# First batch's spectral rows moved inside SBUF, convolution sums seeded in PSUM, transposes in one pass: a Fourier and mlp kernel on one core

## The chip, the cores and the metric

The kernel runs on one core of one Trainium2 chip, in one launch. The metric is the device time of one execution in microseconds (us). Times were taken over three runs of the kernel before: median 1088.05, lowest 1087.7, highest 1088.87. One further execution was profiled; its span is 1087.9 us, and all durations below come from it.

The core has five engines that work from instruction streams of their own: TensorE (PE; its weight loads are listed as PEld), VectorE (DVE), ScalarE (ACT), GpSimd (POOL), and SyncE (SP), which here issues the transfers. Each runs its instructions in a fixed order and waits on semaphores for the others. Matmul results land in PSUM banks; everything else lives in SBUF or in DRAM.

## The reference, cut to what matters

```python
def _attn_ref(x, weight_gen):               # B=8, S=4224, D=192, H=8 heads, K=7 taps
    w = exp(weight_gen - max); w = w / (sum(w) + 1e-09)        # softmax over the taps
    x_pad = np.concatenate([np.zeros((B, K - 1, D)), x], axis=1)
    x_unf = x_pad[:, np.arange(S)[:, None] + np.arange(K)[None, :], :].reshape(B, S, K, H, D // H)
    return np.einsum('bshk,bskhg->bshg', w, x_unf).reshape(B, S, D)

def _moe_ref(x, w_ch1, w_ch2):
    X = np.fft.fft(np.fft.fft(x, axis=1), axis=2)
    u = x + np.real(X)
    un = (u - mean(u)) / np.sqrt(var(u) + 1e-06)               # over the last axis
    return u + np.maximum(un @ w_ch1, 0.0) @ w_ch2             # 192 -> 768 -> 192
```

The second function is applied to what the first returns. Everything is fp32 in and out.

## The kernel before

A batch of 4224 rows is held as 128 partitions by 33 rows of 192 values. The 33 rows are cut into eight chunks of four rows (0 to 7) and one chunk (8) of one row; after the transform the rows are worked on in nine groups. A batch goes through these stages:

- `conv` (`wide_conv` from batch 2 on): the softmax of the taps, and for each chunk seven products of the input rows with the tap weights and their sum. In batch 0 chunks 0, 1, 3, 5 and 7 are summed on TensorE: each product tile `pr` is multiplied by an fp32 identity into a pair of PSUM banks `pa` (L767, and L732 for the products that ACT makes, L723), and ACT copies the banks to `u` (L779). The other chunks and batches add `pr` to `u` on POOL or DVE (L771). The constants `PE_SUMS`, `ACT_TAPS`, `POOL_TAPS`, `DVE_ADDS` say which engine makes and adds which tap; batch 0's chunks are taken in the groups `[(8,0), (1,2), (3,4), (5,6), (7,)]`.
- `fold` (L794, L795) adds two mirrored halves of a chunk into `sm` on POOL. `spectrum` takes a 128-point transform of `sm` on TensorE (`pg`, L803), ACT copies a part (`up`), and DVE writes sums and differences as `gt` (L810, L813). `gt` has 128 partitions, the cosine and sine parts of 65 frequencies. SP stores it in DRAM as `g_d` (L816, L817).
- `transform` loads `g_d` back in pieces `g` of four frequency triples, 102 partitions each (L889, L891), and takes the 33-point transform on TensorE (`pp`, L899); ACT copies the result to `pq`.
- `mix`: for each group four pairs of matmuls (`eo`, L930), a copy on ACT (`ot`), and four DVE operations that add the result to `u` (L936 to L939).
- `norm`: for the first three groups of batch 0 (`QUICK = 3`) the statistics come from DVE (L960, L961), ACT normalises (`un`, L976), TensorE transposes by a matmul with the fp32 identity (`tr`, L986), ACT copies the high half to fp16 (`ht`, L987), and DVE subtracts for the low half (L989). For all other groups POOL makes the two halves (`hl`, L1001, L1003), and a DMA transposes them (L1006).
- `mlp`: `ph` (L1060) is the first matmul into 768 columns, ACT and DVE evict it with the relu, `po` (L1094) is the second, and DVE evicts it onto `u` (L1099). Group g of batch 0 has `po_g_0` and `po_g_1`, one for each half of its rows. The weights are loaded and split into fp16 parts (batch 0's weight preparation: `words_to_f32`, L472 to L483, and `split_f32`, L488, L489, on ACT and DVE).

Nothing of this is scheduled by hand. `kernel` traces all instructions once, `plan` gives each a price by `cost` (TensorE by columns and passes, a transfer by its issue, its landing and its queue time), and `walk` lists them: at each step the instruction that opens next on its engine, ranked by what hangs behind it. The result is one static order for each engine, so a changed price or a changed instruction shifts the order of much else. Warm-up matmuls (`keep_warm`) are put where TensorE has nothing else; `WARM` says after which group and how many.

The tables of the 33-point transform (`te`, `to`) and of the 128-point transform (`f1`) fix in which partition a frequency lands.

## Time and profile before

| | |
|---|---|
| median of 3 runs | 1088.05 us (1087.7 to 1088.87) |
| span of the profiled execution | 1087.9 us |
| TensorE busy / weight loads | 1065.5 / 802.9 us |
| DVE, ACT, POOL busy | 958.7, 800.0, 857.1 us |
| granted TensorE clock, mean | 0.998 |
| TensorE idle, 0 to 60 us | 9.2 us |
| TensorE idle, 200 to 1000 us | 3.5 us |
| first `ph` of group 0 | at 100.68 us |
| first instruction that issues the store of the last `gt` of batch 0 | at 71.45 us |

The profiled execution ran 0.15 us shorter than the median. Of the stages, batch 0's convolution lasts to about 71 us, its transform to 90, and its first mlp matmul begins at 100.7. The convolution of batch 1 lies beside batch 0's mlp and ends on POOL at 199.6 us. From there to 1000 us TensorE is idle less than 1% of the time.

A row of a timeline gives the start and the length in us, the engine, the line, the operation, what it writes and reads, how many such instructions follow one another, and in brackets the idle time before the first of them and what ended it. A row of a group of instructions gives the count, the busy time in us, the mean duration of one in ns, and the idle time before them. Rows of waits give total us, times, longest.

### The profile page before, as it was taken

What the parts mean: (1) busy time and instruction counts of PE and PEld (TensorE: products, weight loads), DVE (VectorE), ACT (ScalarE), POOL (GpSimd) and SP (SyncE); (2) the same over time, 40 slices, a digit from 0 to 9 for tenths busy, and PEclk for the clock granted to TensorE, in tenths of its full rate; (3) what the DMA queues carried; (4) which work ended last, traced back from release to release, by engine and by line L of the source; (5) the groups of instructions that cost most, each with busy time, mean ns of one, the idle gap of its engine ahead of it and who ended that gap; (6) DMA issues with size and microseconds to landing.
All of it is one profiled execution on the core that took longest, in us unless ns stands there. A gap on an engine that the chain in (4) does not pass through costs nothing.

```text
span 1087.9 us, 23453 instructions
## 1 busy us (share of the span) xinstructions
PE 1065.5 (98%) x8600; PEld 802.9 (74%) x8600; DVE 958.7 (88%) x1639; ACT 800.0 (74%) x2414; POOL 857.1 (79%) x615
## 2 busy tenths in 40 slices
PE   7899999999999999999999999999999999999998
PEld 5477777787767877777778876887778777786767
DVE  8999999899989999899999999899999998355543
ACT  4666864679966878788786877678786878588842
POOL 5989699899969999799969999699969999011200
PEclk9999999999999999999999999999999999999999
DMA  9353135714492348623582348624582333623311
GB/s 323 129 146 115 34 94 141 202 46 111 119 259 80 85 115 206 170 67 85 129 248 79 92 109 220 157 57 121 122 205 68 83 68 89 140 56 76 79 53 48
DMA packets 171091, 131.20 MB, mean 121 GB/s; under 512 B 119067, under 2 KB 151776, under 8 KB 170976
## 3 DMA queue, kind: packets, MB, share of 16 engines
q1 hardware_dynamic: 170976, 129.70, 45.2%
q8 instruction: 68, 1.11, 0.4%
q14 instruction: 47, 0.39, 0.1%
HBM read 61.46 MB, written 39.37 MB: 93 GB/s over the span
## 4 chain that ended last, share of the span: by engine, by line
PE 66%; DVE 14%; POOL 5%; DMA 4%; ACT 3%; issue 3%; SPq 0%; DVEq 0%; ACTq 0%; POOLq 0%
PE po L1094 27%; PE ph L1060 24%; PE pp L899 5%; PE eo L930 4%; PE ph L1027 3%; DVE pr L847 3%; POOL u L771 2%; PE pg L803 2%; DVE hh L1080 2%; ACT pr L723 1%; DMA ht<-hl 1%; DVE pr L762 1%; POOL u L851 1%; DMA g<-g_d 1%; DMA ring<-ht 1%
## 5 line engine op out<-in xcount | busy, mean ns | idle before, releaser
L851 POOL TENSOR_TENSOR u<-u,pr 128x1536 f32<-128x1536 f32 x144 | 497.0, 3452 | 5.5 <-DVE pr L847 1.7
L1094 PE MATMUL po<-w2h,hh 128*128 128x192 f16 x2832 | 409.2, 247 | 0.0
L1094 PEld LDWEIGHTS <-hh 128*128 128x128 f16 x4248 | 359.1, 98 | 60.1 <-issue 15.2
L1060 PE MATMUL ph<-ht,w1h 128*128 128x512 f16 (+1 forms) x1296 | 382.7, 362 | 0.3 <-ACT ht L987 0.3
L1094 PE MATMUL po<-w2l,hh 128*128 128x192 f16 x1416 | 348.8, 246 | 0.0
L1080 DVE SCALAR_TENSOR_TENSOR hh<-ph,hh 128x512 f16<-128x512 f32 (+1 forms) x390 | 240.5, 636 | 60.9 <-ACT hh L1079 60.5
L1079 ACT ACTIVATE hh<-ph 128x512 f16<-128x512 f32 (+1 forms) x390 | 206.0, 550 | 89.2 <-PE ph L1060 41.0
L847 DVE TENSOR_TENSOR pr<-x_sb,wp 128x1536 f32<-128x1536 f32 x144 | 249.7, 1747 | 7.3 <-POOL u L851 7.3
L1060 PEld LDWEIGHTS <-w1h 128*128 128x128 f16 x1296 | 125.3, 98 | 97.9 <-issue 9.4
L1060 PE MATMUL ph<-ht,w1l 128*128 128x512 f16 (+1 forms) x528 | 181.7, 350 | 0.0
L996 ACT ACTIVATE un<-u,rs 128x192 f32<-128x192 f32 x252 | 122.2, 539 | 40.2 <-POOL rs L994 34.5
L1001 POOL TENSOR_TENSOR hl<-un,hl 128x512 f16<-128x512 f32 (+1 forms) x69 | 74.9, 1086 | 84.3 <-issue 42.5
L771 POOL TENSOR_TENSOR u<-u,pr 128x768 f32<-128x768 f32 (+1 forms) x72 | 117.9, 1649 | 12.2 <-DVE pr L762 11.4
L967 ACT ACTIVATE junk<-u,st 128x192 f16<-128x192 f32 x252 | 114.3, 453 | 4.4
L965 ACT ACTIVATE junk<-u 128x192 f16<-128x192 f32 x252 | 90.8, 360 | 27.6 <-DVE u L939 21.8
L1099 DVE SCALAR_TENSOR_TENSOR u<-po,isc,u 128x384 f32<-128x384 f32 (+1 forms) x122 | 73.1, 599 | 21.1 <-PE po L1094 20.7
L930 PEld LDWEIGHTS eo<-cs_sb,pq 97*128 97x128 f32 x544 | 78.3, 191 | 13.4 <-issue 4.4
L930 PE MATMUL eo<-cs_sb,pq 97*128 97x97 f32 x544 | 85.7, 275 | 0.0
L762 DVE TENSOR_TENSOR pr<-x_sb,wp 128x768 f32<-128x768 f32 (+1 forms) x91 | 74.7, 868 | 2.1 <-POOL u L771 0.7
L1060 PEld LDWEIGHTS <-w1l 128*128 128x128 f16 x528 | 51.9, 98 | 21.6 <-issue 0.5
L794 POOL TENSOR_TENSOR sm<-u 128x382 f32<-128x382 f32 x64 | 64.6, 1009 | 3.7 <-ACT u L779 3.2
L994 POOL TENSOR_TENSOR rs<-st,rs 128x4 f32<-128x4 f32 (+1 forms) x69 | 13.6, 201 | 67.4 <-DVE rs L970 67.3
(130 smaller groups left out, 1538.4 us busy)
## 6 DMA issues: line engine op xcount, KB each, us to landing
out_dram<-u SPq DMA_DIRECT2D x64, 384.0 KB
x_sb<-in_x_dram SPq DMA_DIRECT2D x48, 384.0 KB
g<-g_d SPq DMA_DIRECT2D x40, 336.0 KB
x_sb<-in_x_dram SPq DMA_DIRECT2D x8, 864.0 KB
g_d<-gt SPq DMA_DIRECT2D x32, 195.0 KB
g_d<-gt SPq DMA_DIRECT2D x32, 189.0 KB
w<-in_weight_gen_dram SPq DMA_DIRECT2D x6, 924.0 KB
x_sb<-in_x_dram SPq DMA_DIRECT2D x8, 672.0 KB
```

What stands on the lines that cost most here:

```text
L762: last_product[b] = nc.vector.tensor_tensor(out=dst, in0=rows, in1=wk, op=ALU.mult)
L771: adder.tensor_tensor(out=u, in0=u, in1=pr, op=ALU.add)
L847: last_product[b] = nc.vector.tensor_tensor(out=pr.rearrange("p (s r) (h g) -> p s (r h) g", s=2, g=G), in0=rows, in1=wp[:, :, :, k:k + 1] ...
L851: nc.gpsimd.tensor_tensor(out=u, in0=u, in1=pr, op=ALU.add)
L930: last_mix[b] = nc.tensor.matmul(eo[:, e, j, :], lhsT=pq[0:DH, e, r, r:r + P], rhs=cs_sb[:, e, :], start=True, stop=True)
L965: nc.scalar.activation(junk, uv[t], AF.Identity, scale=-1.0 / D, accum_out=st[:, t, 0:1])
L967: nc.scalar.activation(junk, uv[t], AF.Square, bias=st[:, t, 0:1], accum_out=st[:, t, 1:2])
L996: nc.scalar.activation(un[:, t, :], uv[t], AF.Identity, bias=rs[:, 1, t:t + 1], scale=rs[:, 0, t:t + 1])
L1060: last_ph[n] = nc.tensor.matmul(ph[:, 0:T], lhsT=wt[:, cs_], rhs=ht[:, 0:T, blk], start=(i == 0 and not opens), stop=(i == len(terms) - 1 ...
L1079: nc.scalar.activation(a[:, 0:T], ph[:, 0:T], AF.Relu)
L1080: nc.vector.scalar_tensor_tensor(out=l[:, 0:T], in0=ph[:, 0:T], scalar=0.0, in1=a[:, 0:T], op0=ALU.max, op1=ALU.subtract)
L1094: nc.tensor.matmul(po[t // 2][:, t % 2, :], lhsT=hx[:, t], rhs=wx[:, c2, :], start=(c2 == 0 and i == 0), stop=(c2 == NH - 1 and i == len(t ...
```

## The change

In batch 0 the `gt` rows are no longer stored in DRAM and loaded again. They go from SBUF to SBUF: 17 transfers of 126 rows by 768 bytes and 18 small ones of one or two rows put them where `transform` reads them, into a part of the tile of batch 1's rows, which is not used yet. For this `u` becomes two fixed tiles (`halves`), the tables are put in the order 6 x 21 frequency rows and 2 left over, and batches 1 to 7 store `g_d` as [22, 6, 17, 192] in two transfers of 126 and 2 rows. The stores of zeros at the start are gone.

For each chunk summed on TensorE DVE's first product is written into the two PSUM banks, in two halves, after small fp16 identity matmuls have opened the banks; before, it was a product in SBUF and two fp32 identity matmuls.

The `norm` transposes of the first three groups use the transpose mode of TensorE. The groups of batch 0 become `[(8,0), (1,2), (3,4), (5,), (6,7)]`; ACT's tap of chunk 7 becomes a DVE product, and the folds of chunks 5 and 7 go to DVE, one operand of them read from PSUM. The warm-up after the last chunk has 18 matmuls in place of 40. `cost` has new prices: transposes of one pass, SBUF to SBUF transfers at 600 ns and 1.5 ns for each piece, slower DVE operations with two SBUF operands.

```diff
-ACT_TAPS = {(0, 1): (0,), (0, 3): (0,), (0, 5): (0,1), (0, 7): (0,)}
+ACT_TAPS = {(0, 1): (0,), (0, 3): (0,), (0, 5): (0,1)}
-WARM = {-1: 14, 7: 40}
+WARM = {-1: 14, 6: 18}
+DVE_FOLDS = (5, 7)
+OPENING = [(8, 0), (1, 2), (3, 4), (5,), (6, 7)]
...
-        t = 2 * max(112 if 64 < n <= DH else 56, 0.855 * n) if reads[0].dtype == F32 else max(55.8, 0.417 * n + 2.4)
+        t = (1 if ins.is_transpose else 2) * max(112 if 64 < n <= DH else 56, 0.855 * n) if reads[0].dtype == F32 else max(55.8, 0.417 * n + 2.4)
...
-        return 400, 2000 + WIRE * count(out) * size, out.ap[0][1] * count(out) / run * (0.5 + 0.0023 * run * size)
+        local = all(ap.tensor.name in sbuf for ap in reads + writes)
+        return 600 + 1.5 * out.ap[0][1] * count(out) / run if local else 400, 2000 + WIRE * min(map(count, reads + writes)) * size, out.ap[0][1] * count(out) / run * (0.5 + 0.0023 * run * size)
...
-        t = 150 + (6.27 if ins.opcode == "Reciprocal" else 1.042) * n + (60 if len(reads) == 3 and n < 512 else 0)
+        slow = len(reads) == 2 and n > 64 and all(ap.tensor.name in sbuf and ap.ap[-1][0] for ap in reads)
+        t = 150 + (6.27 if ins.opcode == "Reciprocal" else 2.0 if slow else 1.042) * n + (60 if len(reads) == 3 and n < 512 else 0)
...
+    halves = [cpool.tile([P, NC // 2, 8, D], F32, name=f"u{i}") for i in range(2)]
+    g0 = halves[1][:, 1:NC // 2].rearrange("p q r d -> p (q r) d")
+    ident16 = ident32.bitcast(F16)[:, 0:P]
...
-                    if i > 0 or pa:
+                    seeds = pa if i == 0 and mine else None
+                    if seeds:
+                        for bank in seeds:
+                            for at_ in range(0, 2 * D, P):
+                                nc.tensor.matmul(bank[:, at_:at_ + P], lhsT=ident16, rhs=ident16, start=(at_ == 0), stop=False)
+                    elif i > 0 or pa:
...
+                        if seeds:
+                            for h in range(2):
+                                last_product[b] = nc.vector.tensor_tensor(
+                                    out=pa[h][:, 0:2 * D].rearrange("p (n g) -> p n g", g=G), in0=rows[:, h], in1=wk[:, h], op=ALU.mult)
...
+                    if pa and c in DVE_FOLDS:
+                        fold(b, sm, pa[0][:, 0:2 * D].rearrange("p (r d) -> p r d", r=2), u[:, 1], nc.vector)
...
-        if at == 2 or c == NC:
+        if b == 0:
+            for j in range(J):
+                last_g2[0] = nc.sync.dma_start(g0[t2 + j:t2 + j + 6 * NT:NT, 0:NM], gt[0:6 * NM, at + j])
+            for kk in range(2):
+                last_g2[0] = nc.sync.dma_start(g0[kk * NT + t2:kk * NT + t2 + J, NM], gt[6 * NM + kk:6 * NM + kk + 1, at:at + J])
+        elif at == 2 or c == NC:
...
-                    nc.tensor.matmul(tr[i][0:m, t, :], lhsT=un[:, t, i * P:i * P + m], rhs=ident32, start=True, stop=True)
+                    nc.tensor.transpose(tr[i][0:m, t, :], un[:, t, i * P:i * P + m], ident32)
```

The first place is SP's order of transfers at the end of batch 0's convolution; before, two stores of the last `gt` and then the loads of the transform:

```order
L816 DMA g_d_95<-gt_4_452 65x768
L817 DMA g_d_95<-gt_4_452 63x768
L816 DMA g_d_95<-gt_6_591 65x768
L817 DMA g_d_95<-gt_6_591 63x768
L889 DMA g_0_0_716<-g_d_95 112x4x192
L889 DMA g_0_4_734<-g_d_95 112x4x192
L889 DMA g_0_8_752<-g_d_95 112x4x192
```

The same place after the change:

```order
L636 DMA x_sb<-in_x_dram 128x768
L846 DMA u_73<-gt_4_473 6x21x192 x4
L846 DMA u_73<-gt_6_658 6x21x192 x4
L848 DMA u_73<-gt_4_473 2x1x192 x4
L848 DMA u_73<-gt_6_658 2x1x192 x4
```

The loads are gone; four long transfers of each of the last two `gt` tiles and eight small ones stand in their place.

The second place is DVE around the first mix rows of group 0 (`eo_0`), which stood behind the preparation of the second weight's parts (`w2f`):

```order
L478 TENSOR_SCALAR pa_w_1_1014<-pw_w_1_1015 128x384
L481 SCALAR_TENSOR_TENSOR t_w_1_1016<-raw_w_416,pa_w_1_1014 128x384
L483 TENSOR_TENSOR w2f<-pw_w_1_1015,t_w_1_1016 128x384
L936 TENSOR_TENSOR eo_0_928<-eo_0_928,ot_0_933 128x2x97
L937 TENSOR_TENSOR eo_0_928<-eo_0_928,ot_0_933 128x194
L938 TENSOR_TENSOR u_0_145<-u_0_145,eo_0_928 128x2x2x97
```

After the change the same engine has:

```order
L486 SCALAR_TENSOR_TENSOR t_w_0_978<-raw_w_432,pa_w_0_976 128x384
L971 TENSOR_TENSOR eo_0_900<-eo_0_900,ot_0_905 128x2x97
L501 SCALAR_TENSOR_TENSOR w1l_90<-pw_w_01_889,sc_w_851,w1h_89 128x384
L972 TENSOR_TENSOR eo_0_900<-eo_0_900,ot_0_905 128x194
L487 TENSOR_SCALAR pa_w_0_976<-raw_w_432 128x384
L973 TENSOR_TENSOR u_72<-u_72,eo_0_900 128x2x2x97
```

The first mix moved ahead of most of that preparation (parts 0 and 1 of the second weight), which now stands between the mix rows.

The third place is TensorE at the first output matmul of group 1 (`po_1_0`). Before, the first `ph` of group 3 stands ahead of it:

```order
L1060 MATMUL ph_2_5_1439<-ht_2_1107,w1l_90 128x512
L1060 LDWEIGHTS w1h_87
L1060 MATMUL ph_3_0_1470<-ht_3_1277,w1h_87 128x512
L1060 LDWEIGHTS w1l_88
L1060 MATMUL ph_3_0_1470<-ht_3_1277,w1l_88 128x512
```

After the change it stands behind it, and `po_1_0` follows directly on the last `ph` of group 2:

```order
L1099 MATMUL ph_2_5_1410<-ht_2_1079,w1l_92 128x512
L1133 MATMUL po_1_0_1302<-w2f,hh_1_0_1176 128x192
L1133 MATMUL po_1_0_1302<-w2f,hh_1_1_1189 128x192
L1133 MATMUL po_1_0_1302<-w2f,hh_1_2_1223 128x192
L1133 MATMUL po_1_0_1302<-w2f,hh_1_3_1237 128x192
```

The five `ph` matmuls of group 3's first columns moved behind `po_1_0`, whose bank DVE must have emptied of group 0 before.

More of the change, by code (lines that the diff above doesn't have):

```diff
@@ L24 @@
 NK1 = 65
+NM = 21
 DH = 97
@@ L32 @@
 QUICK = 3
-BN_GROUPS = ()
+BN_QUICK = 3
+ONE_BIAS = 0
 EPS_ACT = 0
@@ L87, in area @@
     if kind == "psum":
-        return (0, P), [(0, 1)]
-    dims, base, parts, size = [list(d) for d in ap.ap], ap.offset, (0, 1), BYTES[ap.dtype]
+        return (0, P, 1), [(0, 1)]
+    dims, base, parts, size = [list(d) for d in ap.ap], ap.offset, (0, 1, 1), BYTES[ap.dtype]
     if kind != "dram":
-        step, n = dims.pop(0)
-        parts, base = ((base // step, base // step + n), base % step) if step else ((0, P), base)
+        (step, n), pitch = dims.pop(0), int(np.prod(ap.tensor.shape[1:]))
+        first, every = base // pitch, max(step // pitch, 1)
+        parts, base = ((first, first + (n - 1) * every + 1, every), base % pitch) if step else ((0, P, 1), base)
     free, run = [], 1
@@ L114, in meet @@
         return False
+    if pa[2] == pb[2] > 1 and (pa[0] - pb[0]) % pa[2]:
+        return False
     i = j = 0
@@ L171, in plan @@
     writers, readers, users = defaultdict(list), defaultdict(list), defaultdict(list)
-    rows = defaultdict(list)
+    rows, sbuf = defaultdict(list), {name for name, home in homes.items() if home[0] not in ("psum", "dram")}
     for at, ins in enumerate(nc.cur_bb.bb.instructions):
@@ L199, in plan @@
                 needs.setdefault(index[first.name], False)
-        price = cost(ins, lane, reads, writes)
+        price = cost(ins, lane, reads, writes, sbuf)
         if joined:
@@ L652, in conv @@
                 keep_warm(pst("fft", 2, [P, P], F32, "warm_x"), WARM[-1])
-        groups = [(NC, 0), (1, 2), (3, 4), (5, 6), (7,)] if b == 0 else [(c,) for c in range(NC + 1)]
+        groups = OPENING if b == 0 else [(c,) for c in range(NC + 1)]
         if b >= WIDE_FROM:
@@ L726, in conv @@
                 for c, R, u, wp, pa, wq, pt, at in chunks:
-                    order = turns(pt, TURNS[len(pt)]) if pt and pa else range(K)
+                    order = turns(pt, TURNS[len(pt)]) if pa and 0 < len(pt) < K else range(K)
                     order = [k for k in order if k not in at] + list(at)
+                    mine = [k for k in range(K) if k not in pt and k not in at]
+                    if pa and mine:
+                        order.sort(key=lambda k: k != mine[0])
                     k = order[i]
@@ L777, in conv @@
                     n = R * D // 2
-                    for i in range(2):
+                    for i in (1, 0):
                         nc.scalar.copy(u[:, i].rearrange("p r d -> p (r d)"), pa[i][:, 0:n])
@@ L976, in norm @@
                     nc.scalar.activation(un[:, t, :], uv[t], AF.Identity, bias=rs[:, 1, t:t + 1], scale=rs[:, 0, t:t + 1])
-            for t in range(ACT_ROWS, T):
+            for t in range(ACT_ROWS, T) if not ONE_BIAS else ():
                 nc.vector.tensor_scalar(out=un[:, t, :], in0=uv[t], scalar1=st[:, t, 0:1], scalar2=rs[:, 0, t:t + 1],
```

133 lines of the change are left out of this document (70 added, 63 removed).

## The prediction

> **What bounds the kernel now.** I read the page's busy times first, then busy time by stretch, and then the chain of waits of the first 135 us, since every edit sits there.
>
> ```profile
> PE 1065.5 (98%) x8600; PEld 802.9 (74%) x8600; DVE 958.7 (88%) x1639; ACT 800.0 (74%) x2414; POOL 857.1 (79%) x615
> ```
> ```profile
> 30.00:60.00 30.00, 26.94 (x86) 15.23 (x87) 29.90 (x48) 23.49 (x108) 29.59 (x23) 1.00 0.42 130
> 120.00:140.00 20.00, 18.64 (x105) 13.91 (x104) 19.90 (x35) 16.80 (x52) 15.98 (x11) 1.00 0.21 50
> 160.00:200.00 40.00, 37.65 (x209) 29.01 (x208) 38.76 (x73) 23.38 (x60) 39.86 (x36) 1.00 0.48 148
> 200.00:400.00 200.00, 198.89 (x1659) 153.58 (x1658) 188.02 (x297) 154.95 (x469) 185.88 (x115) 1.00 0.49 126
> ```
>
> The columns are PE, weight load, DVE, ACT, POOL, granted clock, DMA share and GB/s. From 200 us on TensorE idles about 1 us in 200: there only less TensorE work, or an earlier arrival, counts. The change leaves the work of batches 1 to 7 as it is, so the end moves by how much earlier TensorE arrives there. From 30 to 60 us DVE is full (29.90 of 30); from 160 to 200 us POOL (39.86 of 40) and DVE (38.76) are.
>
> ```profile
> 51.79 7.39 ACT pr L723 x36
> ...
> 91.55 0.56 DVE w2f L483
> ...
> 97.18 2.85 PE tr L986 x14
> ...
> 100.68 1.24 PE ph L1060 x5
> ...
> 122.91 0.96 DVE pr L762
> ...
> 123.94 1.82 POOL u L771
> ```
>
> The chain of waits (start, length, what) runs through ACT's tap products, DVE's weight words, the transposes and the first mlp matmul at 100.68, then through DVE to POOL's adds of batch 1.
>
> **The end of batch 0's convolution.** Groups of the first 125 us (busy us, mean ns of one, idle before) and two neighbours of DVE's timeline (start, length):
>
> ```profile
> L762 DVE TENSOR_TENSOR pr<-x_sb,wp 128x768 f32<-128x768 f32 x46 | 41.2, 948 | 1.3 <-PE pa L767 0.7 <-DMA x_sb<-in_x_dram 0.5
> L723 ACT ACTIVATE pr<-x_sb,wa 128x24 f32<-128x24 f32 x160 | 33.9, 303 | 5.1 <-DVE wa L715 4.7 <-DMA x_sb<-in_x_dram 0.5
> L767 PE MATMUL pa<-pr,ident 128*128 128x384 f32 x120 | 44.1, 511 | 7.0 <-DVE pr L762 6.8 <-POOL pr L760 0.2
> L794 POOL TENSOR_TENSOR sm<-u 128x382 f32<-128x382 f32 x10 | 10.0, 1004 | 3.2 <-ACT u L779 3.2
> 92.82 0.56 DVE L938 TENSOR_TENSOR u<-u,eo 128x388 f32<-128x388 f32 x1
> 93.29 0.54 DVE L939 TENSOR_TENSOR u<-u,eo 128x380 f32<-128x380 f32 x1
> ```
>
> ACT loses 32 of its 160 tap products, 32 x 33.9/160 = 6.8 us. DVE takes one more product, about 0.85 us of engine time (of 0.948 with its latency: at 137.14, further below, two of them are followed by the next row at 138.84). Two folds move from POOL (-2.2) to DVE: 0.47 (the next row starts 0.47 after 92.82) and some 0.07, so +1.1. Each of five seeds splits a 768 product into two of 384, 2 x 0.47 - 0.85 = 0.09, so +0.4 in all. For that, ten fp32 identity matmuls go on TensorE, 20 passes at 44.1/120 = 7.3 us, and 30 small fp16 ones come, whose cost no row shows: between nothing and the 128x128 fp32 pass of the warm-up row further below (3.81/24 = 0.16) each, 0 to 4.8. I take 2.4, the middle; so TensorE's load falls here, and its 6.8 us of waits for DVE's products hide the rest at either end. Sum for DVE: 0.85 + 1.1 + 0.4, **+2.3 us of work**, against stalls that go (0.7 for the product tiles by its row, and some 0.5 around ACT) and batch 1's softmax pieces that now stand behind the last rows. Adding the durations of DVE's rows in the new order puts the last transform rows at 69.1 written, 2.3 sooner than now:
>
> ```profile
> 71.08 0.34 DVE L813 TENSOR_TENSOR gt<-pg,up 128x190 f32<-128x190 f32 x1
> 71.45 0.30 SPq L816 DMA_DIRECT2D g_d<-gt  x1
> 75.43 10.54 SPq L889 DMA_DIRECT2D g<-g_d  x6
> 86.75 2.08 SPq L516 DMA_DIRECT2D w1h<-w1h  x2
> ```
> ```profile
> SPq L889 <- DMA g_d<-gt: 3.1, 1, 3.1
> 79.56 0.87 PE L899 MATMUL pp<-te_sb,g 102*97 102x102 f32 x8
> 89.95 2.21 PE L930 MATMUL eo<-cs_sb,pq 97*128 97x97 f32 x16
> 92.02 0.36 DVE L936 TENSOR_TENSOR eo<-eo,ot 128x194 f32<-128x194 f32 x1
> ```
>
> **The transfer.** Now it is two hops: issued 71.45 and 71.80, landed near 75.2 (3.1 us of waiting), loads from 75.43, first pp at 79.56. One hop is thus 3.3 to 4.1 us. After the change two long issues follow the last rows; the trace has no such shape. Bounds: 0.3 each as the stores (71.45), or twice the 1.04 of an SBUF to SBUF issue over 64 partitions (86.75, x2) because there are 126. So pp begins between 69.1 + 0.6 + 3.3 = 73.0 and 69.1 + 4.2 + 4.1 = 77.4. I take 0.62 each, as the later w1h issues go, and 4.1: **74.5**. The small two-row transfers follow, and only the last pp pair, 9 us on, needs them. From first pp to DVE's first mix row is 92.02 - 79.56 = 12.5 at most, and 11.5 at least (half of the eo group, 89.95 + 1.1); at 11.8 mix can begin at 86.3. DVE's own rows, added up, reach it at 86.2, as 4.6 us of word preparation now stands behind it and 1.2 of stalls went. So mix begins some 5.7 earlier than 92.02.
>
> The Trainium skill, "DMA: Bandwidth & Descriptors", section "Why a DMA increments its semaphore by 16 and not by 1", speaks against this: a transfer is spread over the largest number of engines up to 16 that divides the slowest dimension of both sides. With 126 partitions read and 6 partition groups written that is 6 engines, by the 16-engine rate of the page's table an estimated 1 us more for the last pair, hence 75.5. No run here shows that split; the trace's bounds contain it.
>
> **Norm, transposes, mlp start.** Between first mix and first transposed group DVE's work grows from 7.9 to 13.6 us, as word preparation is interleaved. That returns most of it.
>
> ```profile
> 97.18 3.19 PE L986 MATMUL tr<-ident,un 128*128 128x128 f32 x16 [0.28 <-ACT un L976]
> 100.66 0.69 DVE L989 TENSOR_TENSOR ht<-tr,ht 128x512 f16<-128x512 f32 x1 [0.47 <-ACT ht L987]
> ```
>
> Sixteen passes take 3.19 us, 0.2 each; eight take 1.6. The first ph then starts near 96.9 (now 100.68); DVE's ht subtraction comes at 99.8 (now 100.66); TensorE then waits 2.8 us for the second group's norm. At the end of the third group's transposes I get 2.4 us of TensorE lead, 1.2 of it from the single pass there. A single pass not taken would cost those 1.2; a price below zero is excluded, since no instruction is added.
>
> **Where the lead goes.** POOL waits 8.41 us for DVE's second chunk 2 product and is then full until 199.6:
>
> ```profile
> 123.94 1.82 POOL L771 TENSOR_TENSOR u<-u,pr 128x768 f32<-128x768 f32 x1 [8.41 <-DVE pr L762]
> 202.68 1.16 POOL L1001 TENSOR_TENSOR hl<-un,hl 128x512 f16<-128x512 f32 x1 [2.83 <-DMA ht<-hl]
> ```
>
> DVE's total to that product is unchanged: 2.3 us more work, 2 to 2.7 of stalls gone, so 123.0 to 123.8 against 122.91. Batch 1's convolution therefore ends at about 199, 0.6 sooner at best by the order of POOL's adds. Meanwhile TensorE is sent to the first output matmul of group 1 (po_1_0) before group 3's first ph, and it needs DVE to evict group 0:
>
> ```profile
> 137.14 1.78 DVE L762 TENSOR_TENSOR pr<-x_sb,wp 128x768 f32<-128x768 f32 x2
> 138.84 0.61 DVE L1099 SCALAR_TENSOR_TENSOR u<-po,sc_w,u 128x384 f32<-128x384 f32 x1
> 139.59 4.14 PE L1094 MATMUL po<-w2f,hh 128*128 128x192 f32 x24 [1.36 <-DVE u L1099]
> ```
>
> Now that wait is 1.36. After, TensorE arrives at 134.1 to 134.6 (2.4 of lead, and the 1.1 us of ph moved behind) and the eviction stays at 138 to 139.5, so it resumes at 139 to 140 after **4 to 6 us**. Against now, TensorE is 0.4 late and owes 1.1: -1.5. It gets back what it waits later in this stretch:
>
> ```profile
> PE po L1094 <- DVE u L1099: 2.2, 2, 1.4
> PE pg L803 <- POOL sm L795: 1.3, 1, 1.3
> PE me_w L456 <- ACT un L996: 0.9, 1, 0.9
> ```
>
> 2.2 - 1.4 + 1.3 + 0.9 and 0.3 of smaller ones make 3.3: +1.8 in sum. So long an idle also costs clock:
>
> ```profile
> 10.36 8.09 PE L767 MATMUL pa<-pr,ident 128*128 128x384 f32 x19 [3.87 <-DVE pr L762]
> 2.69 3.81 PE L538 MATMUL warm_x<-ident 128*128 128x128 f32 x24
> 12.00:13.00 1.00, 1.00 (x3) 0.64 (x2) 1.00 (x1) 0.55 (x4) 0.20 (x1) 0.50 1.06 389
> 15.00:16.00 1.00, 1.00 (x4) 0.57 (x3) 1.00 (x3) 1.00 (x6) 1.00 (x1) 1.00 1.03 399
> ```
>
> An idle of 3.87 before 10.36 is followed by a clock of 0.50 until about 15, some 3.4 us at half rate or 1.7 lost. At 4 to 6 us the same can happen: 0 to -1.7, and I take -0.8, as the bottom of my span is where the trace's idle already did it and the top rests on a sum of DVE rows.
>
> The Trainium skill, "TensorE: Matmul & The Clock Gate", Part 1, has the gate watch free-running windows of about 3.4 us, so an idle of 4 to 6 us is caught or not by where it falls. The trace agrees with the length (3.87 caught); by the page alone the sum would be 1087.8 when caught and 1086.1 when not.
>
> For batch 1 to begin sooner its normalised rows must too: its loads stand ahead of a transpose on SP now, and POOL fills the 2.83 us wait shown, worth 2 to 2.8. So that side allows 2.6 to 3.4, and TensorE is the later: 1.8 - 0.8 = **1.0 us gained**. Against the span of 1087.9 (the median is 1088.05, the highest 1088.87) that is 1086.9 for the span, **1087.0** for the median. About 0.2%, 2.2 us, is what a measurement can tell from no change.
>
> **Rivals.** *Lead kept.* If DVE evicts group 0 some 2 us sooner (stalls I have not counted as going, an add on POOL's side), the idle shrinks under 3.9, no clock is lost, and batch 1's 2.6 to 3.4 plus up to 1.2 of work taken from TensorE is gained: 1083.4 to 1085.3. For: DVE's rows in this stretch came 0.8 us quicker than my sum. Against: POOL's 39.86 of 40.
>
> *Late rows, slower.* DVE runs in a fixed order and now has mix in front of word preparation. If pp begins at 77.4 mix opens at 89.2 and DVE stands 3.0 us; the chunk 2 product then comes at 126 to 127, POOL ends 2.6 to 3.2 later and the 8.41 wait grows. With batch 1's loads late by the same, little of the 2 to 2.8 is left: 1090.3 to 1091. It decides from about pp at 76.4. For: the 1.04 us issues; against: the hop of 3.3.
>
> *Not what it says.* If transposes still take two passes, the 1.2 us of lead go and the time is about 1088.
>
> **How the numbers follow.** Forecast 0.39, two passes 0.05 (both within 0.2%), lead kept 0.40 (faster), late rows 0.16 (slower). That is faster 0.40, same 0.44, slower 0.16. The forecast's own range is 1086 to 1088.7; leaving out 1 in 10 on either side, with the lower price widened by the 1.7 of clock, gives 1082.3 to 1090.4.
>
> **What would show it.** pp starting at 73 to 77.4; first mix on DVE at 86 to 87; transposes as half as many instructions; first ph near 97; TensorE waiting 4 to 6 us for an L1138 eviction near 134 to 140, with a clock under 1 behind it; conv 1 on POOL ending near 199. Wrong if POOL's chain begins well before 122, or if pp is later than 77.4.

## The result and the profile after

| | before | after |
|---|---|---|
| median of 4 runs, us | 1088.46 (1087.7 to 1091.69) | 1101.6 (1100.69 to 1102.77) |
| span of the profiled execution, us | 1087.9 | 1099.4 |
| mean granted clock | 0.998 | 0.991 |

The changed kernel takes 1.0117 times as long (95% interval 1.0101 to 1.0133), some 12.7 us more. 1087.0 was forecast, in a range to 1090.4. The page's line of busy times, for the kernel after:

```profile
PE 1063.1 (97%) x8542; PEld 797.3 (73%) x8542; DVE 962.0 (88%) x1648; ACT 795.7 (72%) x2400; POOL 854.8 (78%) x610
```

The shares hardly move. What moves is seen by stretch (start:end, length, busy time of PE, weight load, DVE, ACT and POOL with their instructions, clock, DMA share, GB/s). First the kernel before:

```profile
0.00:60.00 60.00, 50.83 (x168) 30.28 (x169) 55.08 (x90) 34.59 (x146) 46.75 (x46) 0.97 0.65 220
60.00:130.00 70.00, 67.98 (x449) 53.25 (x448) 66.32 (x159) 47.20 (x137) 57.67 (x44) 1.00 0.32 95
130.00:200.00 70.00, 65.50 (x363) 50.23 (x362) 68.55 (x115) 44.83 (x127) 69.86 (x58) 1.00 0.45 128
200.00:1000.00 800.00, 796.49 (x6866) 606.83 (x6865) 728.12 (x1200) 626.90 (x1884) 674.02 (x454) 1.00 0.48 121
```

The same stretches of the kernel after:

```profile
0.00:60.00 60.00, 49.80 (x187) 31.30 (x187) 54.51 (x94) 33.87 (x143) 45.46 (x45) 0.94 0.68 230
60.00:130.00 70.00, 58.34 (x357) 41.14 (x357) 66.47 (x163) 44.23 (x116) 56.37 (x40) 0.95 0.18 53
130.00:200.00 70.00, 65.08 (x349) 50.71 (x349) 62.68 (x104) 38.00 (x108) 68.83 (x56) 0.95 0.49 134
200.00:1000.00 800.00, 793.65 (x6796) 603.38 (x6795) 730.66 (x1197) 622.35 (x1881) 673.37 (x453) 1.00 0.47 120
```

Up to 200 us TensorE stands 11.1 us more (184.3 us busy before, 173.2 after), and its clock takes some 10.6 us of the rest (0.06 x 60 + 0.05 x 70 + 0.05 x 70) where it took 1.8. That is 19.9 us less done. The change took some 10 to 12 us of work from it, an estimate: busy time less what the mean clock took is 1065.5 - 2.2 before and 1063.1 - 9.9 after, 10.1 apart, and every form of matmul counted at its median step from start to start gives 12. Of this 4.7 us are warm-ups (9.4 us busy before, 4.7 after), which nothing waits for. So TensorE comes to 200 us about 9 us behind. From 200 to 1000 us it stands another 2.8 us more. Together that is, within the rounding of the clock, the difference of the spans, 11.5: **up to 200 us TensorE's idle grew by as much as its work fell, and the clock lost came on top.**

The front, as rows of the kernel after's timeline (start, length, engine, line, what, and in brackets the idle before and what ended it):

```profile
69.48 0.34 DVE L843 TENSOR_TENSOR gt<-pg,up 128x190 f32<-128x190 f32 x1
65.20 6.88 SPq L846 DMA_DIRECT2D u<-gt  x8
75.36 0.91 PE L934 MATMUL pp<-te_sb,u 102*97 102x102 f32 x8 [1.56 <-DMA u<-gt]
79.70 0.62 DVE L501 SCALAR_TENSOR_TENSOR w1l<-pw_w,sc_w,w1h 128x384 f16<-128x384 f32 x1 [1.99 <-ACT w1h L500]
88.37 0.36 DVE L971 TENSOR_TENSOR eo<-eo,ot 128x194 f32<-128x194 f32 x1
95.81 2.34 PE L1025 MATMUL tr<-ident,un 128*128 128x128 f32 x8 [1.85 <-ACT un L1015]
98.61 0.59 PE L1099 MATMUL ph<-ht,w1h 128*128 128x512 f16 x1 [0.46 <-ACT ht L1026]
124.28 1.81 POOL L798 TENSOR_TENSOR u<-u,pr 128x768 f32<-128x768 f32 x1 [3.17 <-DVE pr L789]
129.82 0.40 PE L1133 MATMUL po<-w2f,hh 128*128 128x192 f32 x1 [1.64 <-ACT ot L970]
139.88 1.41 PE L1133 MATMUL po<-w2f,hh 128*128 128x192 f32 x7 [0.52 <-DVE u L1138]
```

The first pp is 4.2 us earlier than before, the first mix row 3.65, the first ph 2.07 (79.56, 92.02, 100.68 before); POOL's chain of batch 1 begins 0.34 later, and the wait at po_1_0, the row at 139.88, is 0.52. Ahead of it TensorE stands 1.64 us at 129.82 until ACT has made an `ot` copy, a wait that the kernel before doesn't have. By 110 us TensorE is 1.2 us behind. The clock between, in windows of the kernel after:

```profile
96.00:98.00 2.00, 1.91 (x8) 0.79 (x7) 2.00 (x6) 1.43 (x5) 2.00 (x2) 0.68 0.00 0
98.00:100.00 2.00, 1.17 (x3) 0.26 (x2) 2.00 (x11) 1.29 (x3) 2.00 (x2) 0.50 0.00 0
100.00:102.00 2.00, 1.39 (x4) 0.45 (x4) 2.00 (x8) 0.96 (x3) 2.00 (x2) 0.50 0.00 0
102.00:104.00 2.00, 2.00 (x11) 1.11 (x10) 1.94 (x6) 1.44 (x4) 2.00 (x3) 0.62 0.00 0
```

Then the turn-over from batch 0's last groups to batch 2's convolution, DVE and who waits for it, kernel after:

```profile
182.95 0.35 DVE L840 TENSOR_TENSOR gt<-pg,up 128x194 f32<-128x194 f32 x1
183.22 1.81 DVE L789 TENSOR_TENSOR pr<-x_sb,wp 128x768 f32<-128x768 f32 x2
...
185.85 0.35 DVE L843 TENSOR_TENSOR gt<-pg,up 128x190 f32<-128x190 f32 x1
186.12 0.55 DVE L973 TENSOR_TENSOR u<-u,eo 128x388 f32<-128x388 f32 x1
186.59 0.54 DVE L974 TENSOR_TENSOR u<-u,eo 128x380 f32<-128x380 f32 x1
...
186.35 1.62 PE L833 MATMUL pg<-sm,f_sb 128*128 128x192 f32 x4 [2.27 <-DVE gt L843]
...
187.16 0.36 ACT L1000 ACTIVATE junk<-u 128x192 f16<-128x192 f32 x1 [4.78 <-DVE u L974]
...
203.28 0.20 POOL L1033 TENSOR_TENSOR rs<-st,rs 128x4 f32<-128x4 f32 x1 [3.38 <-DVE rs L1005]
207.14 3.45 POOL L886 TENSOR_TENSOR u<-u,pr 128x1536 f32<-128x1536 f32 x1 [3.67 <-DVE rs L1005]
...
212.56 7.14 DVE L501 SCALAR_TENSOR_TENSOR w2l<-w2f,sc_w,w2h 128x384 f16<-128x384 f32 x3
```

The kernel before at this place:

```profile
179.79 0.35 DVE L810 TENSOR_TENSOR gt<-pg,up 128x194 f32<-128x194 f32 x1
180.06 0.34 DVE L813 TENSOR_TENSOR gt<-pg,up 128x190 f32<-128x190 f32 x1
180.32 0.53 DVE L939 TENSOR_TENSOR u<-u,eo 128x380 f32<-128x380 f32 x1
180.88 0.36 ACT L965 ACTIVATE junk<-u 128x192 f16<-128x192 f32 x1 [1.50 <-DVE u L939]
194.26 2.00 DVE L489 SCALAR_TENSOR_TENSOR w2l<-w2f,sc_w,w2h 128x384 f16<-128x384 f32 x3
```

There the two gt rows and the last mix row stand together, and POOL's idle was the one 2.83 quoted in the prediction. Now the gt row's second half and the mix rows stand behind four products (two of 128x768, two of 128x192); TensorE waits 2.27 for the one (and runs at 0.77 of the clock from 180 to 190), ACT 4.78 for the other, and POOL 7.05 in two pieces for what follows from them.

### The profile page after: what moved, and what is told of

Its sections match the earlier page's. It is cut to its first block, busy times and chain, and to the rows that moved or that the text cites. A ratio compares the mean times of both kernels' runs of the same rounds, so it can differ in the third digit from the quotient of the medians.

```text
span 1099.4 us, 23384 instructions
## 1 busy us (share of the span) xinstructions
PE 1063.1 (97%) x8542; PEld 797.3 (73%) x8542; DVE 962.0 (88%) x1648; ACT 795.7 (72%) x2400; POOL 854.8 (78%) x610
## 4 chain that ended last, share of the span: by engine, by line
PE 71%; DVE 15%; DMA 6%; ACT 3%; POOL 3%; issue 2%; SPq 0%; DVEq 0%; POOLq 0%; ACTq 0%
PE po L1133 29%; PE ph L1099 25%; PE eo L965 4%; PE pp L934 4%; PE ph L1066 4%; PE pg L833 3%; DVE pr L789 3%; DMA ht<-hl 3%; POOL u L798 2%; DVE pr L882 2%; DMA g<-g_d 2%; PE pa L794 1%; DVE w2l L501 1%; ACT pr L736 1%; DVE hh L1119 1%
## 5 line engine op out<-in xcount | busy, mean ns | idle before, releaser
L1099 PEld LDWEIGHTS <-w1h 128*128 128x128 f16 x1296 | 125.8, 99 | 103.9 <-issue 11.5
L1040 POOL TENSOR_TENSOR hl<-un,hl 128x512 f16<-128x512 f32 (+1 forms) x69 | 74.5, 1080 | 82.1 <-ACT hl L1039 41.8
L789 DVE TENSOR_TENSOR pr<-x_sb,wp 128x768 f32<-128x768 f32 (+1 forms) x87 | 71.0, 859 | 4.4 <-POOL u L798 3.5
L1033 POOL TENSOR_TENSOR rs<-st,rs 128x4 f32<-128x4 f32 (+1 forms) x69 | 13.6, 200 | 73.5 <-DVE rs L1005 69.7
L1133 PE MATMUL po<-w2f,hh 128*128 128x192 f32 x336 | 62.8, 329 | 2.2 <-ACT ot L970 1.6
```

What stands on the lines that cost most here:

```text
L789: last_product[b] = nc.vector.tensor_tensor(out=dst, in0=rows, in1=wk, op=ALU.mult)
L1099: last_ph[n] = nc.tensor.matmul(ph[:, 0:T], lhsT=wt[:, cs_], rhs=ht[:, 0:T, blk], start=(i == 0 and not opens), stop=(i == len(terms) - 1 ...
L1133: nc.tensor.matmul(po[t // 2][:, t % 2, :], lhsT=hx[:, t], rhs=wx[:, c2, :], start=(c2 == 0 and i == 0), stop=(c2 == NH - 1 and i == len(t ...
```

## The experiments

A ratio is to the kernel before on the same chip, with its 95% interval. "Lag" is how much later a kernel has as much TensorE work left as the kernel before has at a given time (forms at their median steps). The lag at 130 us thus reaches to some 134 to 138 us of a changed kernel's own time. In the kernel after it is 1.2 us at 110, 3.8 at 130, 3.0 at 180, 6.8 at 200 and 11.5 at 1000; at 200 this is 2 us less than the sum over the stretches above, as not every step takes its median. A lag is read from one profiled execution: of t9, t12 and t13 it was the slowest, of t10 the fastest.

**Parts of the change alone, on the kernel before.** Single-pass transposes with every other instruction in its place (t1_one_pass), the new prices alone (t3_new_prices), and, as a measure of what any new order does, one price moved by 3% (t4_jitter_before); on the kernel after, the old prices (t2_old_prices). Of the prices, which are all of the function cost, one is shown; they also include a lower one for POOL's products with a broadcast operand (1.78 in place of 2.13 ns an element).

```diff
 t1_one_pass, on the kernel before
-nc.tensor.matmul(tr[i][0:m, t, :], lhsT=un[:, t, i * P:i * P + m], rhs=ident32, start=True, stop=True)
+nc.tensor.transpose(tr[i][0:m, t, :], un[:, t, i * P:i * P + m], ident32)
 t3_new_prices, on the kernel before; t2_old_prices is the reverse on the kernel after
-        t = 150 + (6.27 if ins.opcode == "Reciprocal" else 1.042) * n + (60 if len(reads) == 3 and n < 512 else 0)
+        slow = len(reads) == 2 and n > 64 and all(ap.tensor.name in sbuf and ap.ap[-1][0] for ap in reads)
+        t = 150 + (6.27 if ins.opcode == "Reciprocal" else 2.0 if slow else 1.042) * n + (60 if len(reads) == 3 and n < 512 else 0)
...
 t4_jitter_before, on the kernel before
-WIRE = 0.7
+WIRE = 0.72
```

> The kernel before with one edit: the 24 transposes of the first three groups in transpose mode; every engine's order is that of before, row for row. Theory A (single-pass transposes let TensorE's clock fall, as in the changed kernel's 0.50 at 98 to 102 us): granted clock under 0.9 somewhere between 97 and 112 us, and a time of 1089 to 1092. Rival B (transposes are harmless, the clock fell there for the idle ahead of them): clock 1.00 throughout 97 to 112 and 1086.5 to 1088.5, as 24 passes of 0.18 to 0.2 us go.

> The changed kernel with all its edits but the planner's prices of before. Theory P (the order that the new prices make costs the time): 1088 to 1093. Rival E (the edited instructions themselves cost it, whatever the order): 1099 to 1104.

> The kernel before, no instruction changed, planned with the prices of the changed kernel. Theory P: 1094 to 1101, slower by half of the loss or more. Rival E: 1086 to 1090.

> The kernel before with one planner constant moved by 3% (WIRE 0.70 to 0.72, a transfer's landing), so that the order changes in many places and no instruction does. If any re-planning of a tuned order costs several us (theory S, scatter): 1091 to 1098. If orders are worth about the same (rival): 1087 to 1090.

t1: 1089.58 us, ratio 1.0001 (0.9985 to 1.0017). The transposes are harmless there, and worth nothing: the lag is -2.4 at 110 us and -0.9 at 200 us. t3: 1094.7, ratio 1.0054 (1.0033 to 1.0076). t4: 1092.51, ratio 1.0033 (1.0016 to 1.005). Both came as the theories of order and scatter said, t3 at the low edge. t2: 1599.06, ratio 1.469, which neither theory had; its order is another one altogether, with this as the largest of TensorE's waits (total, times, longest), so it compares with nothing, and why the old prices lead there stays open:

```profile
PE pp L932 <- DMA g<-g_d: 186.2, 11, 36.5
```

The kernel before's own instructions in another order cost 3.6 and 5.9 us. Two rows of t4 and one of t3 show the form of it, a stall of over 2 us where there was none, and the clock behind it:

```profile
130.48 1.79 PE L1094 MATMUL po<-w2f,hh 128*128 128x192 f32 x6 [2.29 <-DVE gt L813]
130.00:140.00 10.00, 9.52 (x43) 7.66 (x44) 9.59 (x17) 7.62 (x25) 10.00 (x8) 0.83 0.47 98
```
```profile
186.83 0.59 PE L1096 MATMUL po<-w2f,hh 128*128 128x192 f32 x2 [3.48 <-DVE m_w L452]
```

**One row, or some warm-ups, at the stalls shown.** In t5_pairs each second gt row goes directly behind its first in DVE's order; in t6_warm_fill 7 and 8 warm-ups without a price fill the stalls of the first mix; t7_both has both; nothing else moves. t8_jitter_after is the kernel after with one price moved by 3%.

```diff
 t5_pairs, in plan, on the kernel after
+    order["dve"] = [x for ins in order["dve"] if ins.name not in seconds
+                    for x in ([ins, seconds[PAIRS[ins.name]]] if ins.name in PAIRS else [ins])]
 t6_warm_fill, behind the keep_warm calls of the first mix
+            for _ in range((7, 8)[g - 1]):
+                more = nc.tensor.matmul(warm, lhsT=ident32, rhs=ident32, start=True, stop=True).ins
+                glued.add(more.name)
+                FREE.add(more.name)
 t8_jitter_after
-WIRE = 0.7
+WIRE = 0.72
```

> The changed kernel with each second gt row (the difference) put directly behind its first (the sum) in DVE's queue; all other orders and instructions as they are. Theory C (at 182 to 193 us TensorE stands 0.8 and 2.3 us, the second for a gt row that stands 2.9 us behind its partner, and then runs at half clock): the stall of 2.27 goes or falls under 1, the clock from 184 to 193 is 1.00, and 4 us come back: 1096.5 to 1098.5. Rival (POOL sets the pace there, so an earlier TensorE only waits later): 1100.5 to 1102.

> The changed kernel with 7 and 8 more warm-up matmuls behind the two sets between the eo groups of the first mix; no other row of any engine moves. Theory C: TensorE's idle of 1.55 and 1.85 us at 89.5 and 94 us is filled, the clock is 1.00 from 96 to 104, and the first group's transposes and ph matmuls take half as long. If that lead lasts: 1097 to 1099. If the later waits for DVE take it back, as a lead of this stretch was taken back in the changed kernel: clock 1.00 but 1100 to 1102. Rival A (transposes don't keep the clock up): clock still 0.5 near 98 to 102.

> Both edits together. Theory C: the sum of the two gains, 1093 to 1097. Rival (bound by POOL and DVE): 1100 to 1102.

> The changed kernel with WIRE 0.72 in place of 0.70, as was done to the kernel before. Theory S (the order is a draw, and that of the changed kernel is a bad one): 1091 to 1098, that is 4 us or more off 1101.6. Rival (the edits cost the time in any order): 1099 to 1104.

1102.27 (ratio 1.0113, 1.0087 to 1.014), 1104.91 (1.0127, 1.0096 to 1.0159), 1103.28 (1.0117, 1.0082 to 1.0151) and 1100.97 (1.0095, 1.006 to 1.0129): none gives anything back beyond the intervals. In t5 the 2.27 us at pg falls to 0.25, and the next row of DVE that stands behind the products takes its place:

```profile
187.84 0.92 PE L839 MATMUL pg<-sm,f_sb 128*128 128x192 f32 x4 [0.25 <-POOL sm L831]
190.70 0.69 PE L972 MATMUL eo<-cs_sb,pq 97*128 97x97 f32 x4 [1.62 <-DVE u L981]
```

In t6 the clock stays at 1.00 through the first mix and falls at 103 us instead of 97. And in all four profiles TensorE ran out of warm-ups 2 us or more ahead of the first pp, which the kernel after's own profile does not show so strongly. The next runs follow both leads.

**The mix rows, the warm-ups ahead of pp, the transposes.** t9_mix_first moves L843, L973 and L974 of 185.85 to 187.1 directly behind 182.95; t10_warm_pp adds 12 warm-ups ahead of the first pp; t11_mix_warm does both; t12_two_pass writes the transposes as two-pass matmuls again, at the price of one; t13_all does all of these and fills the mix as t6. Every other instruction keeps its place.

```diff
 t9_mix_first, in plan; MOVED holds the names of L840 (anchor), L843, L973, L974
+    late = [ins for ins in order["dve"] if ins.name in rest]
+    order["dve"] = [x for ins in order["dve"] if ins.name not in rest
+                    for x in ([ins] + late if ins.name == anchor else [ins])]
 t10_warm_pp, in keep_warm
+        for _ in range(12 if count == WARM[6] else 0):
+            more = nc.tensor.matmul(spare, lhsT=ident32, rhs=ident32, start=True, stop=True).ins
+            glued.add(more.name)
+            FREE.add(more.name)
 t12_two_pass
-                    nc.tensor.transpose(tr[i][0:m, t, :], un[:, t, i * P:i * P + m], ident32)
+                    ONE.add(nc.tensor.matmul(tr[i][0:m, t, :], lhsT=un[:, t, i * P:i * P + m], rhs=ident32, start=True, stop=True).ins.name)
```

> The kernel after with three VectorE rows moved and nothing else: the second gt row of batch 1's groups 4 and 5 (L843 at 185.85) and the two mix additions of batch 0's group 7 (L973, L974 at 186.12 and 186.59) go directly behind the first gt row at 182.95, ahead of the products of batch 1's chunks 7 and 8. Turn-over theory (the loss between 180 and 250 us is one chain: these rows stand behind products, TensorE stands 2.27 us for gt, the clock halves behind it for 3.3 us, ScalarE stands 4.78 us for the mix rows, and norm, softmax of batch 2 and GpSimd follow): the moved rows are written near 184.5, TensorE's stand at that pg falls under 0.8, the wait at the eo matmuls that took its place when the gt row alone was moved does not come, the clock of 180 to 200 is at least 0.95, ScalarE's norm begins about 2.5 us sooner, and 3 to 6 us come back: 1095.5 to 1098.5. Scatter theory (a new order has waits everywhere, and the one shown only happens to be the largest): the products, 1.3 us later, make GpSimd and then TensorE wait elsewhere, and the time stays within 1.5 us of 1101.6.

> The kernel after with 12 more fp32 warm-up matmuls (0.16 us each, 1.9 us) directly behind the 18 that precede the first pp, without a price, so that every other instruction keeps its place. Warm-up theory (with 18 in place of 40 TensorE runs dry before pp in many executions, and pp, pq, ScalarE's casts and the first mix rows come late at half clock): the idle ahead of the first pp is under 0.5 us, the clock of 74 to 90 is 1.00, the first pp starts at 75.4 to 77.4 as in the executions profiled so far, VectorE's first mix row comes at 88.4 or before, and 1 to 2 us come back: 1099.5 to 1100.5. Rival (VectorE and GpSimd set the pace to 200 us, so a lead of TensorE here is waited away later): within 0.8 us of 1101.6.

> Both edits of the two runs before together. Turn-over and warm-up theories: the gains add, 4 to 8 us, 1093.5 to 1097.5. If only the turn-over counts: as the first of the three runs, 1095.5 to 1098.5. Scatter theory: within 1.5 us of 1101.6.

> The kernel after with the 24 transposes of the first three groups written as fp32 matmuls again (two passes each), priced as one pass so that every instruction keeps its place. Idle-transposes theory (single-pass transposes do not keep the clock up: in the kernel after, 1.85 us of idle, 2.34 us of transposes and 0.46 us of idle follow one another from 93.96, and the clock is 0.50 from about 97 to 103): the clock of 96 to 104 is 1.00, the 1.2 us of added passes are less than the some 3 us saved, and TensorE's lag at 110 to 130 us is 1 to 3 us less. Rival (the two stalls of 1.55 and 1.85 us before them suffice): the clock falls at 96 to 97 as before, and the time is 0 to 1.5 us longer.

> The edits of t9_mix_first, t10_warm_pp and t12_two_pass together, and 7 and 8 more warm-ups without a price in the two stalls of the first mix; all other instructions stand as in the kernel after. If turn-over and clock account for the early loss: clock 1.00 from 70 to 130 and from 180 to 200, TensorE at 200 us no more than 2 us behind the kernel before (some 7 in the kernel after), 1094 to 1097 in sum; what is then left is lost after 200 us in small waits. If they do not: 1098 or more, as t9_mix_first.

| | median, us | ratio | lag at 180 | lag at 200 |
|---|---|---|---|---|
| after | 1101.6 | 1.0117 (1.0101 to 1.0133) | 3.0 | 6.8 |
| t9_mix_first | 1098.76 | 1.0093 (1.0064 to 1.0122) | 7.7 | 8.7 |
| t10_warm_pp | 1107.51 (1100.07 to 1108.21) | 1.0153 (1.0108 to 1.0198) | 4.0 | 6.7 |
| t11_mix_warm | 1098.4 | 1.0093 (1.006 to 1.0125) | 5.0 | 6.0 |
| t12_two_pass | 1106.7 | 1.0151 (1.0109 to 1.0193) | 6.4 | 10.7 |
| t13_all | 1100.69 | 1.0099 (1.007 to 1.0129) | 5.9 | 8.1 |

The turn-over did as its theory said inside the trace: where the mix rows are moved, the stretch of 180 to 200 us costs 1.0, 1.0 and 2.2 us of lag (t9, t11, t13) instead of 3.8, 2.7 and 4.3 (after, t10, t12), and in t9 the clock of that stretch is 1.00. The rest of its forecast, 3 to 6 us of the time, came at best by half: t9's median is 2.8 us under that of the kernel after, with intervals that overlap. The warm-ups ahead of pp removed the idle there and gave no time. t10's profiled execution is its fastest; the other three took 7 to 8 us longer at a mean clock of 0.983 to 0.986 instead of 0.989, which is 3 to 7 us of it, and no profile shows where. t12 answers its own question, in the windows and rows of its profile:

```profile
98.00:100.00 2.00, 1.65 (x9) 0.98 (x8) 2.00 (x8) 1.99 (x5) 2.00 (x2) 0.92 0.00 0
100.00:102.00 2.00, 1.73 (x10) 1.07 (x9) 2.00 (x8) 0.73 (x3) 2.00 (x3) 1.00 0.00 0
102.00:104.00 2.00, 1.18 (x4) 0.29 (x3) 2.00 (x10) 1.06 (x3) 2.00 (x2) 1.00 0.00 0
98.53 3.19 PE L1028 MATMUL tr<-ident,un 128*128 128x128 f32 x16 [0.35 <-ACT un L1018]
```

With two passes the clock is back at 1.00 during the transposes, and in t13 it is 1.00 from 70 to 130 us; with one pass it halves during them (after, from 97) or behind them (t6, from 103). Yet t13's lag grows from 4.3 at 110 to 8.3 at 130, by more than that of the kernel after (1.2 to 3.8). At 131 us, between those two lags, TensorE stands 1.64 us until ACT's `ot` copy is made, and this time the clock halves behind it:

```profile
130.00:140.00 10.00, 8.36 (x39) 6.96 (x39) 8.63 (x17) 7.82 (x26) 9.92 (x7) 0.83 0.26 55
```

The same 1.64 us stand in the kernel after and in t6, t9, t10, t11, t12 and t18; no run moved that copy. t13 was to come within 2 us of the kernel before at 200 us if turn-over and clock were the early loss. It is 8.1 behind, so they are not all of it.

**Parts of the change undone, all planned anew.**

```diff
 t14_dram_rows: the branches on b == 0 of spectrum and transform
-        if b == 0:
+        if False:
 t15_no_seeds
-                    seeds = pa if i == 0 and mine else None
+                    seeds = None
 t16_old_opening
-DVE_FOLDS = (5, 7)
-OPENING = [(8, 0), (1, 2), (3, 4), (5,), (6, 7)]
-ACT_TAPS = {(0, 1): (0,), (0, 3): (0,), (0, 5): (0,1)}
-WARM = {-1: 14, 6: 18}
+DVE_FOLDS = ()
+OPENING = [(8, 0), (1, 2), (3, 4), (5, 6), (7,)]
+ACT_TAPS = {(0, 1): (0,), (0, 3): (0,), (0, 5): (0,1), (0, 7): (0,)}
+WARM = {-1: 14, 7: 40}
 t17_no_slow, in cost
-2.0 if slow else 1.042
+1.042
```

> The kernel after with batch 0's rows stored in DRAM and loaded again as in the kernel before, all else as after, planned anew. If the SBUF rows themselves cost (their long issues, what they push aside): 1088 to 1093. If the loss lies in how the instructions of the later stretches are ordered, and a lead at the first pp is lost anyway: first pp 2 to 4 us later than in the kernel after, but the time within 4 us of it, 1098 to 1106, with its largest TensorE stalls again between 120 and 200 us, at other places.

> The kernel after without seeds: the first product of each chunk that TensorE sums is a product in SBUF and two fp32 identity matmuls again, all else as after, planned anew. If the seeds cost: 1088 to 1094. If order decides: within 4 us of the kernel after, 1097 to 1106, though TensorE has 7 us more work in the first 70 us.

> The kernel after with the opening of the kernel before: the same groups of chunks, ScalarE's tap of chunk 7, the folds of chunks 5 and 7 on GpSimd, 40 warm-ups behind chunk 7; SBUF rows, seeds, single-pass transposes and prices as after, planned anew. If the new opening carries the loss: 1088 to 1094, with no half clock ahead of the first pp. If any plan of the new instructions loses it: 1097 to 1106, with 10 us or more of TensorE idle between 70 and 200 us, at places of its own.

> The kernel after without the higher price of VectorE operations on two SBUF operands (1.042 ns an element for all, as in the kernel before), all else as after, planned anew. If this price carries the loss that the new prices made in the kernel before (5.9 us): 1094 to 1097. If no single price does: 1097 to 1106.

1107.36 (ratio 1.0159, 1.0129 to 1.0189), 1098.88 (1.0081, 1.0051 to 1.011), 1101.02 (1.0129, 1.0086 to 1.0171) and 1097.48 (1.0087, 1.0057 to 1.0116). No single part carries the loss: whichever is undone, 9 to 17 us stay; t14 is even above the range that was given for it. Between 70 and 200 us their stalls of over 2 us lie at other places than in the kernel after, some of them shared: ahead of the first pp 4.76 (t14) and 2.75 (t15); at 116 to 118, behind ACT's hh, 2.51 (t14), 2.82 (t15) and 2.70 (t17); 2.09 at 119 and 2.65 at 128 in t16; at 183 to 186, behind DVE's m_w, 2.78 (t14) and 3.16 (t16), where t3 has its 3.48. Whether several parts undone together would give the time back was not tried.

**The mix rows where the kernel before has them.** The last run goes further than t9.

```diff
 t18_mix_as_before, in plan; the anchor is the eviction L1138 of po_2_1, PAIR the gt rows as in t9
+    rest = {MOVED[k] for k in ("minus", "plus", "low", "high", "rs")}
+    late = [ins for ins in order["dve"] if ins.name in rest]
+    order["dve"] = [x for ins in order["dve"] if ins.name not in rest and ins.name != PAIR[1]
+                    for x in ([ins] + late if ins.name == MOVED["anchor"] else [ins] + gt if ins.name == PAIR[0] else [ins])]
```

> The kernel after with six VectorE rows moved: the four mix rows of batch 0's group 7 (182.29 to 186.59) go directly behind the second eviction of group 2 (169.68), near where the kernel before has them (172.18 to 180.32) and where their input ot has lain since 168.6; with them the reciprocal of group 6's norm (187.51); and the second gt row of groups 4 and 5 goes behind the first, as in t9_mix_first. Turn-over theory: ScalarE's norm of group 7 begins before 182 in place of 187.16, TensorE's lag does not grow by more than 1.5 us from 180 to 200, batch 2's Exp begins 2 to 3 us sooner behind the DVE row that releases it, GpSimd's two idles of 3.38 and 3.67 shrink to under 5 us in sum, and 4 to 7 us come back: 1094.5 to 1097.5. Scatter theory: within 1.5 us of t9_mix_first (1098.8) or worse.

1102.97 (1099.09 to 1107.84), ratio 1.0128 (1.0103 to 1.0153): the time did not come back. In its trace the turn-over's cost to TensorE is gone, the lag goes from 8.9 at 180 to 8.9 at 200, and the clock of that stretch is 1.00:

```profile
180.00:190.00 10.00, 8.09 (x42) 5.34 (x41) 9.93 (x15) 2.45 (x6) 10.00 (x8) 1.00 0.44 125
190.00:200.00 10.00, 9.49 (x55) 7.75 (x55) 9.27 (x19) 7.38 (x22) 10.00 (x12) 1.00 0.87 275
```

But the 8.9 were there at 180 already, since in this execution the first pp came at 79.16 and POOL's chain began at 130.35; and behind 200 us the next thing on the chain of waits, POOL's wait and DVE's w2l, stands as in the kernel after:

```profile
209.23 3.46 POOL L896 TENSOR_TENSOR u<-u,pr 128x1536 f32<-128x1536 f32 x1 [3.69 <-DVE rs L1017]
...
214.73 7.08 DVE w2l L509 x3
```

**The front, across the profiles.** In the kernel after, nine variants with its order of the other rows up to that place, and t8 with an order of its own:

| | first pp | first mix on DVE | batch 1 begins on POOL |
|---|---|---|---|
| before | 79.56 | 92.02 | 123.94 |
| after | 75.36 | 88.37 | 124.28 |
| t10_warm_pp | 76.38 | 89.34 | 125.25 |
| t11_mix_warm | 77.40 | 90.36 | 126.29 |
| t8_jitter_after | 77.32 | 91.56 | 129.51 |
| t5_pairs | 77.45 | 91.86 | 127.78 |
| t6_warm_fill | 76.83 | 92.10 | 128.03 |
| t7_both | 77.43 | 91.66 | 127.58 |
| t9_mix_first | 77.79 | 93.07 | 128.98 |
| t12_two_pass | 76.83 | 91.09 | 127.70 |
| t13_all | 77.52 | 90.48 | 127.07 |
| t18_mix_as_before | 79.16 | 94.43 | 130.35 |

POOL's chain begins 35.9 us after the first mix row, 36.6 with two-pass transposes (t12, t13), 38.0 in t8; before it was 31.9. Where pp starts without an idle ahead of it (t10, t11, t13) the first mix row follows 13.0 us behind, where 3 us of idle have halved the clock 15.3 (t6, t9, t18). A late first pp is passed on in full.

## Why the prediction was wrong

1. *The transfer* (pp at 74.5, bounds 73.0 to 77.4). The last gt row was written at 69.82 against 69.1. The issues were mis-sized: 8 take 6.88 us, 0.86 each instead of 0.62, in one queue, and the last long one ends at 72.08. pp began at 75.36, within the bounds; but in other executions of the same order it began up to 79.16, so the upper bound was too low, and 77.4 was no rare end: in seven of the eleven rows above pp is within 0.1 us of it or later. Two of its terms vary. From the end of the last long issue to pp it takes 3.3 to 5.1 us, not 3.3 to 4.1. And the last gt row goes with the clock of 0 to 60 us: it is written at 69.7 to 69.9 where that is 0.94 (after, t6, t10) and at 70.8 to 71.7 where it is 0.91 (the other eight). The sum took this stretch at the clock of the kernel before, 0.97.
2. *The first mix row* (86.2). It came at 88.37. The sum of DVE's rows left out a stall of 1.99 us for ACT's w1h, which stands behind the pq copies in ACT's order.
3. *DVE's total to the second chunk 2 product* (123.0 to 123.8). The product began at 123.19 and POOL's add behind it at 124.28: right. The word preparation that moved behind the first mix row, 4.6 us in the prediction's sum, agrees with the 35.9 against 31.9.
4. *Norm and first ph* (half as many transposes, 96.9). The first group's transposes are 8 rows in place of 16, as said, but took 2.34 us instead of 1.6, as the clock fell during them. ph came at 98.61, late by this and item 2.
5. *TensorE's lead, and its wait of 4 to 6 us at po_1_0.* **Failed.** The lead, 3.65 us at the first mix row and 2.07 at the first ph, was spent by 110, not at 134: from 93.96 to 110 TensorE stood 1.85, 0.46, 0.85 and smaller pieces for ACT and DVE and ran at half clock from 97 to 103; then, ahead of po_1_0, came 0.63 and 1.64 for ACT and 0.48 for DVE. TensorE was late at po_1_0, not early, and waited 0.52. The sum followed DVE and took TensorE as ready between the groups, and ACT as never late: the `ot` copy at 129.48 stands in ACT's order behind a normalisation that itself waited 2.25 us for POOL. DVE was full (2.00 of 2 in the windows), so work taken from TensorE there became idle; that it could become nothing else is argued, not shown.
6. *The clock* (-0.8, at 134 to 140). A loss was expected at the wrong stall, and once. The clock halved at 35, at 97 and at 185, and lost some 8.5 to 9 us more than before, about ten times that.
7. *"It gets back what it waits later in this stretch"* (+3.3). **Failed, and with the wrong sign.** The waits of the old order were taken as the only ones that could be there. The new order has its own between 175 and 187: 1.24 for POOL's sm, 0.78 for DVE's m_w, 2.27 behind the split gt rows, and half clock behind that. The lag grew by 3.8 us from 180 to 200, where it should have shrunk; t9 and t18 show by moving rows that this is the place of batch 0's last mix rows and batch 1's gt rows.
8. *Batch 1's normalised rows, 2 to 2.8 us sooner.* **Failed.** conv 1 on POOL ended at 199.3, near the 199 predicted, but then POOL waited 3.38 + 3.67 us instead of 2.83, for reciprocals of DVE. SP's order of transfers, which the step had rested on, did not release it.

Of the rivals, *late rows* had the right direction and a mechanism that most profiles with this order show: pp near or after its 77.4, DVE standing 2 to 6 us for w1h, POOL beginning at 126 to 130. But the kernel after's own profile lost its 11.5 us without it, with pp at 75.36 and POOL at 124.28, so it is not the cause of the loss there. It was given 0.16 and a price of 3 us, and left out the turn-over. *Lead kept* and *two passes* did not happen.

What is shown: the second pass of the transposes (t1) and, with a new plan, the first products' matmuls (t15) were not on the path before 200 us; new orders of the same instructions cost 4 to 6 us by themselves, in two cases (t3, t4); the place of three to six rows of DVE makes 2 to 4 us of TensorE's lag at the turn-over. What is only seen: the 7.14 us of w2l lie on the chain of waits after, 5.1 more than before, 7.15 to 7.16 in every variant with this order of DVE and 7.30 in t8, and 5.22 and 6.98 in t4 and t3, the two reorderings of the kernel before that lost time, against 2.00 in t1, which did not. That is the best candidate for what remains behind 200 us, and moving w2l was not tried. t14 (2.4 us of it, yet the largest ratio of all but t2) and t17 (3.0 us, yet 1.0087) say it cannot be all. So the steps that failed are shown in the traces, but no run gives the time back, and what makes the whole of the 12.7 us stays open. No variant beats the kernel before.
